# Fewer stretches of small products, a third pass one tile later, and five pieces of w_out in three passes

## The chip, the cores and the metric

The kernel runs on one core of one Trainium2 chip. The time is the device time of that core in microseconds. TensorE multiplies, VectorE (DVE in the profile) and ScalarE (ACT) work on the elements, GpSimd (POOL) does almost nothing here, and SyncE (SP) issues the transfers. The kernel before takes 519.27 us, the median of three runs from 519.05 to 519.50 us.

## The reference

Two blocks follow each other. The first is a recurrence over 768 steps, for 4 batches of 8 heads of width 48; its output is the input of a feed-forward layer with a squared ReLU.

```python
for t in range(S):
    state = alpha[:, :, t, :, None] * state + np.einsum('bhd,bhe->bhde', k[:, :, t], v[:, :, t])
    y[:, :, t] = np.einsum('bhd,bhde->bhe', q[:, :, t], state)
x = y.transpose(0, 2, 1, 3).reshape(B * S, H * D)      # 3072 x 384
h = np.maximum(x @ w_in, 0.0)                          # 3072 x 2048
out = h * h @ w_out                                    # 3072 x 384
```

## The kernel before, in words

**The recurrence.** The sequence is cut into 24 blocks of 128 steps, numbered so that block n is chunk n // 4 of batch n % 4. For a block the kernel takes logarithms of alpha (`ln`), sums them along the steps with a product against a triangle (`cs`, in two parts from block 8 on, split by `sp`), and takes exponentials of both signs (`eb`, `ei`), with which q and k are scaled (`mq`, `mk`). TensorE turns q and k by products with the identity (`turn`), and ScalarE copies them out of PSUM (`kc`, `qc`). Then come the small products: `scores` (line 413) and `state_sums` (line 442) for a block, and the output y of a pair of blocks (line 393). y has three parts, the product of q with the two states and a first and a second half of the masked scores times v. The two halves write the same banks from different rows of the array, so an empty POOL instruction, named `passed`, stands between them: it waits for the last product of the first half, and the first product of the second half waits for it. On VectorE a block's scores are masked (`masked`, line 424), its sums are read (`sums_copied`, line 456), and the state is moved on (`next_state`, lines 477 and 479; the last chunk has no next state). For blocks from 16 on each of the last three is two instructions, before that one. `ev_part` copies y out of PSUM into x, the input of the feed-forward layer, in four parts of three copies.

**The feed-forward layer.** Four blocks make a group of 512 rows, and there are six groups, 0 to 5. In group 0 the first layer multiplies in plain fp32. From group 1 on each operand is split into rounded parts and a tile of the hidden layer takes three passes. `in_x` does two of them, six products that end in a ScalarE step on the bank; `in_y` adds the third, three products on the same bank; and `in_post` applies the squared ReLU. A tile is one of three kinds, A, M or D, which set how much of this ScalarE does and how much VectorE. In the loop over the 16 tiles `in_y` runs two tiles behind `in_x`, and `in_post` three behind.

**The second layer** takes w_out in eight pieces. A piece is either plain (`out_plain`, eight fp32 products a group) or goes in three passes (`out_x` with two passes, `out_y` with the third, 24 products a group). `k0` and `k1` are the numbers of three-pass pieces in groups 0 and 1; from group 2 on all eight are. A three-pass piece needs the hidden tiles split first, one ScalarE and two VectorE instructions each (`split_h`, `diff_h`, lines 701, 653, 648).

**The order.** Everything is written by hand in program order. The start is a list of words in `AT['first']`. After it, `weave` walks through the units of the two layers, adds up their costs (about 1.29 us to a unit), and puts an attention step ahead of the first unit that starts at or after the time it is due. The due times of a pair of blocks come from `attention`: turn at t + 6.5, `ga` (sums of the first block, then y of the pair before up to the first half) at t + `AT['ga']`, `gb` (the second half, then sums of the second block) at t + `AT['gb']`. These are three separate stretches of small products a pair. All PSUM tiles come from one pool of eight banks, `ps_att`; a new tile gets the bank that has been free the longest, and waits until its last reader is done. Transfers go down SyncE's queue in program order, and `move` holds one back until an earlier one has landed (`AT['thr']`, `AT['thrp']`).

```python
units.append((1.05, in_x, (n,)))
units.append((0.53, in_y, (n - 2,)))
units.append((0, in_post, (n - AT["post"],)))
```

Of the kernel before, what the change touches and what calls it, by code (L numbers as in the profile page):

```python
# [18 lines left out]


GB = 4
AT = {'thrp': 4.5, 'cvo': 3.35, 'thr': 2.25, 'm48': 16, 'cvs': 3.9, 'cv1': 0.125, 'later': (0, 0, 4, 6, 0, 1, 0), 'evs': 0.1, 'lead': 4, 'post': 3, 'w_first': (46.0, 38.0, 49.0), 'wstep': 1.0, 'w_in_at': 2.5, 'w_in_by': 3.6, 'room1': 22, 'room': 24, 's0': 4, 'ahead': 6, 'late': 2, 'xs': 0.0, 'g0': ((0.5, 4, False, True, 27.75), (25.75, 6, True, True), (29.25, 8, True, False)), 'sc0': (3.25, 2.35, 2.35), 'g1': ((5.5, 8, False, 15.0), (13.0, 10, True), (35.25, 12, True)), 'g': ((2.075, 6, True), (14.25, 8, True)), 'g1x': 51.0, 'gx': 48.75, 'g0x': 56.25, 'k0': 2, 'h0': 15, 'k1': 4, 'h1': 3, 'h1by': 2, 'evs0': 0.7, 'tp': 'ADMD', 'tp1': 'ADAD', 'split': 8, 'o0': (46.5, 48.5), 'o1': (), 'o2': (21.25, 24.75, 24.5, 40.0, 35.25, 28.25), 'str1': 21.5, 'ga': 9.75, 'gb': 12.5, 'cv0': -1.25, 'pre': '1a 0a 0q 0k 1k 1q', 'cp': ('q2a', 'k2b', 'k0a', 'k3a', 'k3b', 'k0b', 'q0b', 'q3b', 'q2b', 'q3a'), 'evd': ((0, 0, 0), (0, 0, 1), (0, 1, 2), (0, 1, 3), (2, 0, 3), (2, 1, 1), (2, 1, 2)), 'first': 'ln0 load1v cs0 ei0 eb0 zeros4 mk0 mq0 qT0 kT0 ln1 cs1 kc0 ei1 warm0 load0v eb1 mk1 qc0 weights0 lt1 sc0 load2a mq1 load2q kT1 kc1 qT1 load2k load3a qc1 load3k kv0 am0 first0 load3v sc1 ln2 kv1 load3q us0 am1 weights6 us1 cs2 ya0 ei2 second0 eb2 lt0 ln3 yb0 load2v mq2 qT2 mk2 load4a ep00 ep01 qc2 kT2 cs3 kc2 eb3 ei3 zeros1 sc2 ep02 mq3 mk3 kT3 ep03 weights2 first1 st0 ha0 second1 lt2 kv2 am2 qT3 load4k kc3 qc3 ha1 weights5 first2 sc3 kv3 am3 load4q us2 ha2 us3 ya2 yb2 weights3 ep20 ep21 ep22 load4v ep23 second2 first3 weights1 st1 weights4 ha3 lt3 hb0 st2 second3 hb2 hb3 hb1 st3'}


RUN = {0: 128, 32: 32, 64: 64, 96: 32}
# [3 lines left out]
def kernel(  # L29
# [12 lines left out]
    nc = tc.nc  # L42
    B, H, S, D = q.shape
# [211 lines left out]
    def work(name, bufs=1):  # L255
        return p2.tile([128, NP, C], FP32, tag=name, name=name, bufs=bufs)
# [279 lines left out]
    def joined(a, n):  # L536
# [28 lines left out]
                    dep(begin, passed)  # L565
        next_state(n + 1)

    def turn(n):

        for m in (n, n + 1):  # L570
            need(("qb", m), ("kb", m))
            given.add(("free", "q", m))
            ps = blk[m]["T"] = [bank(m, "T", (2, NP, 64)) for _ in range(2)]
            for i, x in enumerate("kq"):
                rows = tile_of(x, m).rearrange("a h d -> a (h d)")
                for p in range(NP):
                    for h in range(2):
                        nc.tensor.transpose(  # L578
                            out=ps[h][:, i, p, :], in_=rows[HALF[h], 128 * p : 128 * (p + 1)],
                            identity=ident[HALF[h], HALF[h]],  # L580
                        )

    def turned_copied(x, n):
        t = blk[n][f"{x}s"] = work(f"{x}s", 2 if x == "k" else 4)
        for h in range(2):
            nc.scalar.copy(out=t[:, :, HALF[h]], in_=blk[n]["T"][h][:, "kq".index(x)])

    def ev_part(n, p):
        if p < NP - 1:
# [6 lines left out]
    def ev(n, ps=tuple(range(NP))):  # L596
        g, t = divmod(n, GB)
        need(("y", n))
        if ps[-1] == NP - 1:
            given.add(("x", n))  # L600
        if t == 0 and ps[0] == 0:
            if g == 0:
                xT[g] = [wt("x", shape=(GB * C,)) for _ in range(KM)]
            else:
                x = raw_pool.tile([128, KM, GB * C], FP32, tag="raw", name="x")
                xT[g] = [x[:, kk] for kk in range(KM)]
        x = [x.rearrange("a (t c) -> a t c", c=C) for x in xT[g]]

        for p in ps:
            for e, f, end in ((1, 2 * p * D + 32, 2 * (p + 1) * D), (0, 2 * p * D, (2 * p + 1) * D)):  # L610
                copy = nc.vector.tensor_copy if (n, e, p) in AT["evd"] else nc.scalar.copy
                r = 64 * (e ^ p % 2)
                while f < end:
                    kk, to = divmod(f, 128)
                    m = min(end - f, *(RUN[i % 128] for i in (r, to)))
                    copy(  # L616
                        out=x[kk][to : to + m, t : t + 2],
                        in_=blk[n]["y"][e][r : r + m, :, p // 2],
                    )
                    r, f = r + m, f + m  # L620
        if ps[-1] == NP - 1:
            blk[n].pop("y")
# [146 lines left out]
    def splits_of_x(at, g):  # L769
        return [(at + i * AT["xs"], f, (g, i % KM)) for i, f in enumerate((split_x,) * KM + (diff_x,) * KM)]  # L770

    def layer_in(g):
        units = []
        for n in range(NJ + 2):
            if n < NJ:
                units.append((1.05, in_x, (n,)))
            if 0 <= n - 2 < NJ:
                units.append((0.53, in_y, (n - 2,)))
            if 0 <= n - AT["post"] < NJ:
                units.append((0, in_post, (n - AT["post"],)))  # L780
            if AT["lead"] <= n < AT["lead"] + AHEAD and (g > 1 or AT["k1"] == NW):
                units += splits_of_h(0, n - AT["lead"])
        return units

    AHEAD, MORE = 3, 4
    h_parts, h_diff, extra = {}, {}, []

# [80 lines left out]
                used("d", "o", p)  # L868

    def layer_out(g):  # L870
        posts = [(0, in_post, (n,)) for n in range(NJ + 2 - AT["post"], NJ)] if g else []
        plain = NW - AT["k0"] if g == 0 else NW - AT["k1"] if g == 1 else 0
        first = 2 * plain
        units = [(1, out_plain, (p, t, plain)) for p in range(plain) for t in range(GB)]
        if plain:
            for i, x in enumerate(posts):
                units.insert(1 + 2 * i, x)
            posts = []
        if plain == NW:
            for t in range(GB):  # L880
                units.append((0, lambda t: store(g, t, out_tile(t)), (t,)))
            return units
        ahead = AT["ahead"]
        split = [f for i in range(0 if plain else AHEAD, NJ - first) for f in splits_of_h(first, i)]
        if g == 0:
            split = [f for i in range(NJ - first) for f in [(0, split_h, (first + i, 0)), (0, diff_h, (first + i,))]]
        if plain:
            at = AT["h0" if g == 0 else "h1"]
            for i in range(min(AHEAD, len(split) // 2)):
                units[at:at] = split[0:2]  # L890
# [115 lines left out]
    def attention(t, n0, after, scale=1, begun=True, whole_at=None, turn_at=None):  # L1006
# [41 lines left out]
                        loads(w + later[6], (n + 2, "a"))  # L1048
        return sorted(out, key=lambda x: x[0])

    def weave(units, events, at):
# [74 lines left out]
    for g in range(1, NG):  # L1126
# [52 lines left out]
```

## Time and profile before

| | |
|---|---|
| median of three runs | 519.27 us (519.05 to 519.50) |
| the profiled execution | 520.38 us, of which the span is 518.6 us |
| granted clock of TensorE | 1.000 |
| TensorE busy with products | 507.8 us, 98% of the span |
| VectorE, ScalarE | 355.7 us (69%), 306.4 us (59%) |
| transfers | 102.34 MB, 197 GB/s over the span |

A line of the timeline reads: start, length, engine, source line, operation, what is written from what, shape, and how many records it merges; in brackets the idle time before and what ended it. Matmuls are pipelined, so the length of one is not its price: the price is the distance from one start to the next. An fp32 product has two records, and one on rounded parts has one. In the chain of waits a line is start, length, engine, tile, source line and count.

### The profile page before, as it was taken

What the parts mean: (1) busy time and instruction counts of PE and PEld (TensorE: products, weight loads), DVE (VectorE), ACT (ScalarE), POOL (GpSimd) and SP (SyncE); (2) the same over time, 40 slices, a digit from 0 to 9 for tenths busy, and PEclk for the clock granted to TensorE, in tenths of its full rate; (3) what the DMA queues carried; (4) which work ended last, traced back from release to release, by engine and by line L of the source; (5) the groups of instructions that cost most, each with busy time, mean ns of one, the idle gap of its engine ahead of it and who ended that gap; (6) DMA issues with size and microseconds to landing.
All of it is one profiled execution on the core that took longest, in us unless ns stands there. A gap on an engine that the chain in (4) does not pass through costs nothing.

```text
span 518.6 us, 13019 instructions
## 1 busy us (share of the span) xinstructions
PE 507.8 (98%) x5338; PEld 418.9 (81%) x5338; DVE 355.7 (69%) x628; ACT 306.4 (59%) x649; POOL 5.3 (1%) x29
## 2 busy tenths in 40 slices
PE   7899999999999999999999999999999999999997
PEld 5675455678888669987899988899988899988997
DVE  2766669986887877776697468587465487363861
ACT  4788898547888653485664276772275673164620
POOL 4000000000000000000000000000000000000000
PEclk9999999999999999999999999999999999999999
DMA  9999779472777786898884688864683545699201
GB/s 183 204 267 237 197 189 235 93 228 80 238 190 184 246 243 162 265 279 227 205 225 143 222 247 222 223 200 152 213 274 124 185 121 154 207 380 322 65 2 61
DMA packets 139323, 102.34 MB, mean 197 GB/s; under 512 B 109808, under 2 KB 115968, under 8 KB 139264
## 3 DMA queue, kind: packets, MB, share of 16 engines
q1 hardware_dynamic: 139264, 101.51, 68.2%
q8 instruction: 42, 0.69, 0.6%
q14 instruction: 17, 0.14, 0.1%
HBM read 84.16 MB, written 17.33 MB: 196 GB/s over the span
## 4 chain that ended last, share of the span: by engine, by line
PE 93%; DVE 4%; issue 1%; POOL 1%; ACT 1%; DVEq 0%; POOLq 0%
PE o L809 39%; PE h L726 32%; PE h L919 8%; PE y L393 4%; PE sckv L413 2%; PE T L578 2%; PE sckv L442 2%; PE cs L283 1%; PE cs L286 1%; DVE x L616 1%; PE cs L287 1%; DVE hd L648 1%; DVE hx L653 0%; DVE am L424 0%; ACT x L616 0%
## 5 line engine op out<-in xcount | busy, mean ns | idle before, releaser
L726 PE MATMUL h<-xd,wd 128*128 128x512 f32 x240 | 68.1, 396 | 1.1 <-issue 1.1
L726 PE MATMUL h<-xa,wb 128*128 128x512 f32 x240 | 68.7, 394 | 0.0
L726 PE MATMUL h<-xl,wl 128*128 128x512 f32 x240 | 67.9, 391 | 0.0
L648 DVE TENSOR_TENSOR hid<-h,hid 128x512 f32<-128x512 f32 x40 | 27.6, 689 | 51.1 <-PE h L726 51.0
L616 ACT COPY x<-y 48x256 f32<-48x256 f32 (+3 forms) x133 | 46.7, 365 | 21.2 <-PE y L393 18.8
L809 PE MATMUL o<-wb,ha 128*128 128x384 f32 x160 | 54.5, 340 | 0.0
L743 ACT ACTIVATE h<-h 128x512 f32<-128x512 f32 x40 | 23.3, 582 | 52.3 <-PE h L726 52.3
L809 PE MATMUL o<-wl,hl 128*128 128x384 f32 x160 | 53.7, 336 | 0.1
L809 PE MATMUL o<-wd,hd 128*128 128x384 f32 x304 | 53.7, 334 | 0.0
L809 PE MATMUL o<-w_out,hid 128*128 128x384 f32 x160 | 53.6, 489 | 0.0
L726 PEld LDWEIGHTS h<-xl,wl 128*128 128x128 f32 x240 | 45.1, 188 | 10.1 <-DVE xl L653 0.4
L809 PEld LDWEIGHTS o<-wd,hd 128*128 128x128 f32 x304 | 52.8, 188 | 0.0
L726 PEld LDWEIGHTS h<-xa,wb 128*128 128x128 f32 x240 | 44.4, 188 | 9.8 <-ACT hid L763 0.4
L726 PEld LDWEIGHTS h<-xd,wd 128*128 128x128 f32 x240 | 44.0, 188 | 9.1
L809 PE MATMUL o<-wb,hx 128*128 128x384 f32 x144 | 48.3, 336 | 0.0
L809 PE MATMUL o<-wl,hx 128*128 128x384 f32 x144 | 48.1, 334 | 0.0
L809 PEld LDWEIGHTS o<-w_out,hid 128*128 128x128 f32 x160 | 30.0, 190 | 19.7
L741 ACT ACTIVATE hid<-h 128x512 f32<-128x512 f32 x40 | 24.2, 606 | 32.9 <-PE h L726 32.5
L919 PE MATMUL h<-x,w_in 128*128 128x512 f32 (+1 forms) x120 | 43.4, 512 | 0.2 <-DVE x L616 0.2
L701 ACT ACTIVATE ha<-hid 128x512 fp32r<-128x512 f32 x40 | 25.1, 642 | 20.3 <-PE o L809 7.9
L919 PEld LDWEIGHTS h<-x,w_in 128*128 128x128 f32 x120 | 22.1, 190 | 17.8 <-issue 15.3
L653 DVE SCALAR_TENSOR_TENSOR hl<-ha,hid 128x512 fp32r<-128x512 f32 x40 | 27.5, 687 | 6.9 <-ACT ha L701 6.8
(111 smaller groups left out, 852.5 us busy)
## 6 DMA issues: line engine op xcount, KB each, us to landing
wd<-do SPq DMA_DIRECT2D x36, 384.0 KB
wl<-lo SPq DMA_DIRECT2D x34, 384.0 KB
wl<-li SPq DMA_DIRECT2D x32, 384.0 KB
wd<-di SPq DMA_DIRECT2D x32, 384.0 KB
raw<-in_moe_w_out_dram SPq DMA_DIRECT2D x8, 767.5 KB
raw<-in_moe_w_in_dram SPq DMA_DIRECT2D x8, 767.2 KB
v_in<-in_v_dram SPq DMA_DIRECT2D x24, 192.0 KB
out_dram<-osb SPq DMA_DIRECT2D x24, 192.0 KB
```

The source lines that it names most:

```text
L393: ins = nc.tensor.matmul(out=ys[e][64 * half : 64 * half + D + G * e, m % 2, p // 2, t], lhsT=lhsT, rhs=rhs, start=(half, e) not in seen, ...
L413: nc.tensor.matmul(out=ps[e][HALF[h], 0, p, :], lhsT=ks[rows, p, HALF[h]], rhs=qs[rows, p, HALF[h]], start=True, stop=True, skip_group_che ...
L442: nc.tensor.matmul(out=ps[h][64 * e : 64 * e + m, 1, p, G:64], lhsT=tile_of("k", n)[HALF[h], 2 * p + e, 0:m], rhs=tiles["v"][n % NV][HALF[ ...
L616: copy(out=x[kk][to : to + m, t : t + 2], in_=blk[n]["y"][e][r : r + m, :, p // 2],)
L648: nc.vector.tensor_tensor(out=o, in0=x, in1=z, op=op)
L653: nc.vector.scalar_tensor_tensor(out=o, in0=x, scalar=c, in1=y, op0=ALU.mult, op1=op)
L701: nc.scalar.activation(out=a, in_=x, func=AF.Copy, scale=NEAR * E)
L726: nc.tensor.matmul(out=acc["h", j], lhsT=here[w, "i", p][:, kk, jj * 128 : (jj + 1) * 128], rhs=x_parts[x][:, kk], start=start and kk == 0 ...
L741: nc.scalar.activation(out=hid[j], in_=x, func=AF.Copy, scale=E)
L743: nc.scalar.activation(out=x, in_=x, func=AF.Copy, scale=1.0 + E)
L809: nc.tensor.matmul(out=acc[t][:, 0:DM], lhsT=lhs[:, t * C : (t + 1) * C], rhs=rhs, start=start, stop=stop, skip_group_check=True,)
L919: nc.tensor.matmul(out=ps, lhsT=w[:, kk, c0 : c0 + 128], rhs=xT[g][kk][:, cols], start=(kk == 0), stop=(kk == KM - 1),)
```

## The change

Four parts, all in the order of the work, and one in how many pieces go which way.

1. **Two stretches instead of three.** From group 2 on (`AT['ty']` is 2) a pair that has a pair before it goes through the new `attention_of_two`. `turn_and_y` does y of the old pair up to the first half, then the turn of the new pair, then the second half. `both_sums` does the scores and sums of both new blocks in one stretch, and after it the VectorE steps of both. It touches five pairs (first blocks 14, 16, 18, 20, 22); the last one (24) has no new pair and keeps its two stretches, earlier than before. The four `ev_part`s of a pair, which came 0.1 units apart behind `gb`, start 1.25 or 2.25 units behind the turn and come 1.6 units apart.
2. **The third pass one tile later.** From group 2 on (`AT['lg']` is 2) `in_y` and `in_post` run one tile behind `in_x`. The last third pass of the layer goes behind the first `out_x` of the second layer.
3. **Five pieces of w_out in three passes** in group 1 instead of four (`k1`).
4. **Other order.** The list `first`, the due times, the order of loads, which of the early copies VectorE does (`cp`, `evd`), the kinds of tile, and the limits on transfers under way.

The entries of `AT` that the prediction speaks of:

| entry | before | after |
|---|---|---|
| `k1` | 4 | 5 |
| `lead` (tile at which the first hidden tiles are split) | 4 | 2 |
| `s0` (splits put ahead of the second layer) | 4 | 5 |
| `evs` | 0.1 | 1.6 |
| `g` (pairs of groups 2 to 4: t and first block) | (2.075, 6, True), (14.25, 8, True) | (1, 6, True, 4.0, 1.25), (13, 8, True, 2.125, 2.25) |
| `ga`, `gb` | 9.75, 12.5 | 9.5, 12.5 |
| `gx` (split of the next group's x) | 48.75 | 44.5 |
| `tp` (kinds of four tiles) | ADMD | DMAD |
| `thr`, `thrp` | 2.25, 4.5 | 2.0, 7.0 |
| `cv1` (second step of a weight conversion behind the first) | 0.125 | 3.125 |
| `later` (loads behind ga, gb, turn, cs) | (0, 0, 4, 6, 0, 1, 0) | (0, 3, 1, 12, 3, 0, 1) |
| `o2` (preparing six pieces of w_out in group 1) | (21.25, 24.75, 24.5, 40.0, 35.25, 28.25) | (8.5, 19.25, -2.25, 32.25, 28.25, 39.5) |
| `evd` (early copies of y on VectorE) | (0,0,0) (0,0,1) (0,1,2) (0,1,3) (2,0,3) (2,1,1) (2,1,2) | (0,0,0) (0,0,1) (0,0,2) (0,0,3) (0,1,1) (0,1,3) (2,0,3) (2,1,0) (2,1,1) (2,1,2) |

In the list `first`, `lt0` goes ahead of `cs2`, the loads of block 3's alpha and k ahead of block 2's q and k, `zeros1` (two products that fill time) goes away, and `st1`, `st2` and `ha2` go ahead of the last `yb2`.

```diff
+    def turn_and_y(a, n):
+        if a is not None:
+            product = y_begin(a)
+            for h in range(2):
+                for m, p, e in heads(a):
+                    rows = slice(64 * e, 64 * e + D)
+                    s = blk[m]["u" if h else "s"]
+                    product(m, p, e, s[rows, p, G * (1 - e) : 64], blk[m]["qs"][rows, p, HALF[h]], HALF[h])
+            for m, p, e in heads(a):
+                end = inner(product, m, p, e, e)
+            passed = nc.gpsimd.nop(nofuse=True)
+            dep(passed, end)
+        if n is not None:
+            turn(n)
+        if a is not None:
+            for i, (m, p, e) in enumerate(heads(a)):
+                begin = inner(product, m, p, e, 1 - e)
+                if i == 0:
+                    dep(begin, passed)
+
+    def both_sums(n):
+        for m in (n, n + 1):
+            scores(m)
+            state_sums(m)
+        for m in (n, n + 1):
+            for f in (masked, sums_copied, next_state):
+                f(m)
...
+    def lags(g):
+        return (AT["lag"], AT["post2"]) if g >= AT["lg"] else (2, AT["post"])
+
     def layer_in(g):
         units = []
-        for n in range(NJ + 2):
+        lag, post = lags(g)
+        for n in range(NJ + lag):
+            if n == NJ and lag == 1:
+                left.append(units)
+                units = []
             if n < NJ:
                 units.append((1.05, in_x, (n,)))
-            if 0 <= n - 2 < NJ:
-                units.append((0.53, in_y, (n - 2,)))
-            if 0 <= n - AT["post"] < NJ:
-                units.append((0, in_post, (n - AT["post"],)))
+            if 0 <= n - lag < NJ:
+                units.append((0.53, in_y, (n - lag,)))
+            if 0 <= n - post < NJ:
+                units.append((0, in_post, (n - post,)))
...
         for n in range(first, NJ):
             units.append((1.08, out_x, (n, first)))
+            if left and n == AT["rest"]:
+                units += left.pop()
...
+    def attention_of_two(t, n0, gs=4.0, evy=1.5):
+        out = []
+        later = AT["later"]
+        old, new = n0 - 2, n0 if n0 < NBLK else None
...
+        w = t + 6.5
+        if new is None:
+            out += [(w - 1, ga, (old, None)), (w, gb, (old, None))]
+        else:
+            out.append((w, turn_and_y, (old, new)))
+        for p in range(NP):
+            out.append((w + evy + AT["evs"] * p, ev_part, (old, p)))
...
+        w = t + gs + 6.5
+        out.append((w, both_sums, (n0,)))
...
+                if g >= AT["ty"] and after:
+                    events += attention_of_two(at0 + t, n0, *other)
+                    continue
```

More of the change, by code (lines that the diff above doesn't have):

```diff
@@ new lines @@
+AT = {'tc': 'AAAA', 'rest': 0, 'lg': 2, 'lag': 1, 'post2': 1, 'ty': 2, 'thrp': 7.0, 'cvo': 2.6, 'thr': 2.0, 'm48': 16, 'cvs': 3.55, 'cv1': 3.125, 'later': (0, 3, 1, 12, 3, 0, 1), 'evs': 1.6, 'lead': 2, 'post': 3, 'w_first': (48.25, 39.25, 52.0), 'wstep': 1.6, 'w_in_at': 1.75, 'w_in_by': 3.6, 'room1': 23, 'room': 24, 's0': 5, 'ahead': 9, 'late': 2, 'xs': 0.0, 'g0': ((4.25, 4, False, True, 33.25), (23.75, 6, True, True), (28.0, 8, True, False)), 'sc0': (1.55, 2.35, 2.35), 'g1': ((5.5, 8, False, 16.5), (15.75, 10, True), (32.0, 12, True)), 'g': ((1, 6, True, 4.0, 1.25), (13, 8, True, 2.125, 2.25)), 'g1x': 52.0, 'gx': 44.5, 'g0x': 56.25, 'k0': 2, 'h0': 17, 'k1': 5, 'h1': 4, 'h1by': 2, 'evs0': 0.75, 'tp': 'DMAD', 'tp1': 'MAAD', 'split': 8, 'o0': (45.75, 47.25), 'o1': (), 'o2': (8.5, 19.25, -2.25, 32.25, 28.25, 39.5), 'str1': 21.0, 'ga': 9.5, 'gb': 12.5, 'cv0': 1.125, 'pre': '1a 0a 0q 0k 1k 1q', 'cp': ('k3b', 'k0b', 'q2b', 'k1b', 'q1a', 'q3b', 'k2b', 'k2a'), 'evd': ((0, 0, 0), (0, 0, 1), (0, 0, 2), (0, 0, 3), (0, 1, 1), (0, 1, 3), (2, 0, 3), (2, 1, 0), (2, 1, 1), (2, 1, 2)), 'first': 'ln0 cs0 ei0 eb0 mk0 zeros4 mq0 qT0 kT0 ln1 kc0 load1v cs1 ei1 warm0 eb1 load0v mk1 qc0 lt1 weights0 load2a sc0 load3a kT1 mq1 kc1 load3k qT1 load2q qc1 kv0 am0 us0 sc1 kv1 first0 load2k ln2 load3q lt0 weights6 load2v am1 us1 cs2 eb2 second0 mq2 ya0 ei2 yb0 mk2 ln3 qT2 ep00 ep01 kT2 qc2 cs3 kc2 load3v eb3 sc2 ei3 mq3 weights2 mk3 ep02 kT3 first1 load4q ep03 ha0 qT3 kc3 kv2 qc3 lt2 ha1 st0 second1 am2 us2 sc3 first2 load4a kv3 load4k ha2 weights5 am3 weights3 us3 ya2 st2 st1 weights1 weights4 yb2 ep20 ep21 ep22 ep23 first3 ha3 second2 load4v second3 lt3 st3 hb2 hb0 hb3 hb1'}
@@ L584, in turned_copied @@
         t = blk[n][f"{x}s"] = work(f"{x}s", 2 if x == "k" else 4)
+        i = "kq".index(x)
+        copy = nc.vector.tensor_copy if AT["tc"][2 * (n % 2) + i] == "D" else nc.scalar.copy
         for h in range(2):
-            nc.scalar.copy(out=t[:, :, HALF[h]], in_=blk[n]["T"][h][:, "kq".index(x)])
+            copy(out=t[:, :, HALF[h]], in_=blk[n]["T"][h][:, i])
     def ev_part(n, p):
@@ L610, in ev @@
             for e, f, end in ((1, 2 * p * D + 32, 2 * (p + 1) * D), (0, 2 * p * D, (2 * p + 1) * D)):
-                copy = nc.vector.tensor_copy if (n, e, p) in AT["evd"] else nc.scalar.copy
+                copy = nc.vector.tensor_copy if (n if n < GB else -1, e, p) in AT["evd"] else nc.scalar.copy
                 r = 64 * (e ^ p % 2)
@@ L770, in splits_of_x @@
         return [(at + i * AT["xs"], f, (g, i % KM)) for i, f in enumerate((split_x,) * KM + (diff_x,) * KM)]
+    def lags(g):
+        return (AT["lag"], AT["post2"]) if g >= AT["lg"] else (2, AT["post"])
     def layer_in(g):
         units = []
-        for n in range(NJ + 2):
+        lag, post = lags(g)
[3 more added lines that the diff above has]
+                units = []
             if n < NJ:
                 units.append((1.05, in_x, (n,)))
-            if 0 <= n - 2 < NJ:
-                units.append((0.53, in_y, (n - 2,)))
-            if 0 <= n - AT["post"] < NJ:
-                units.append((0, in_post, (n - AT["post"],)))
+            if 0 <= n - lag < NJ:
+                units.append((0.53, in_y, (n - lag,)))
+            if 0 <= n - post < NJ:
+                units.append((0, in_post, (n - post,)))
             if AT["lead"] <= n < AT["lead"] + AHEAD and (g > 1 or AT["k1"] == NW):
                 units += splits_of_h(0, n - AT["lead"])
+        if left:
+            left.append(units)
+            units = left.pop(0)
         return units
+    left = []
     AHEAD, MORE = 3, 4
@@ L870, in layer_out @@
     def layer_out(g):
-        posts = [(0, in_post, (n,)) for n in range(NJ + 2 - AT["post"], NJ)] if g else []
+        lag, post = lags(g)
+        posts = [(0, in_post, (n,)) for n in range(NJ + lag - post, NJ)] if g else []
         plain = NW - AT["k0"] if g == 0 else NW - AT["k1"] if g == 1 else 0
@@ L877, in layer_out @@
                 units.insert(1 + 2 * i, x)
+            if left:
+                units[1:1] = left.pop()
             posts = []
@@ L1049, in attention, with loads @@
         return sorted(out, key=lambda x: x[0])
+    def attention_of_two(t, n0, gs=4.0, evy=1.5):
+        out = []
+        later = AT["later"]
+        old, new = n0 - 2, n0 if n0 < NBLK else None
+        def loads(at, *which):
+            out.extend((at, load, (m, x)) for m, x in which if m < NBLK)
+        w = t + 6.5
[5 more added lines that the diff above has]
+            out.append((w + evy + AT["evs"] * p, ev_part, (old, p)))
+        loads(w + later[1], (n0 + 2, "v"))
+        loads(w + later[2], (n0 + 3, "v"))
+        if new is None:
+            return sorted(out, key=lambda x: x[0])
+        loads(w + later[4], (n0 + 2, "q"))
+        loads(w + later[5], (n0 + 3, "q"))
+        for at, fs in PLAN:
+            for f in fs.split():
+                if f not in ("turn", "ga", "gb"):
+                    n = n0 + int(f[-1])
+                    out.append((w if f[:2] in ("kc", "qc") else t + at, steps[f[:-1]], (n,)))
+                    if f[:-1] == "cs":
+                        loads(t + at + later[6], (n + 2, "a"))
+        w = t + gs + 6.5
+        out.append((w, both_sums, (n0,)))
+        loads(w + later[0], (n0 + 3, "k"))
+        loads(w + later[3], (n0 + 4, "k"))
+        return sorted(out, key=lambda x: x[0])
     def weave(units, events, at):
```

1 line of the change is left out of this document (removed).

## The prediction

> **What bounds the kernel now.** I read the page first, then the chain of waits in order of time, then TensorE's timeline, and then busy times by stage.
>
> ```profile
> PE 507.8 (98%) x5338; PEld 418.9 (81%) x5338; DVE 355.7 (69%) x628; ACT 306.4 (59%) x649; POOL 5.3 (1%) x29
> PE 93%; DVE 4%; issue 1%; POOL 1%; ACT 1%; DVEq 0%; POOLq 0%
> ...
> 85.11 11.61 PE o L809 x36
> ...
> 237.97 1.11 issue
> ...
> 343.32 30.70 PE o L809 x176
> ```
>
> TensorE is the bound, so a change counts by the TensorE time that it removes and by the waits that it makes. Line 809 gives two prices: 11.61/36 = 0.3225 us for a record of a plain product (two records each) and 30.70/176 = 0.174 us for one product of a three-pass piece. The "issue" line is a wait that nothing in the profile explains; I come back to it.
>
> ```profile
> 307.31 0.84 PE L726 MATMUL h<-xl,wl 128*128 128x512 f32 x3
> 308.09 0.46 PE L578 MATMUL T<-ident,k_in 64*128 64x64 f32 x8
> 308.38 0.41 PE L578 MATMUL T<-ident,q_in 64*128 64x64 f32 x8
> 308.63 0.42 PE L578 MATMUL T<-ident,k_in 64*128 64x64 f32 x8
> 308.89 0.42 PE L578 MATMUL T<-ident,q_in 64*128 64x64 f32 x8
> 309.23 0.97 PE L726 MATMUL h<-xd,wd 128*128 128x512 f32 x3
> 310.04 0.85 PE L726 MATMUL h<-xa,wb 128*128 128x512 f32 x3
> 310.73 0.86 PE L726 MATMUL h<-xl,wl 128*128 128x512 f32 x3
> ```
>
> Here the starts are to be read. Three products take 0.685 us at their pace (310.04 to 310.73). From the due end of the first three (307.31 + 0.685 = 307.995) to the due start of the three after the stretch (310.04 - 0.685 = 309.355) are 1.36 us. The 32 records inside need four times 0.25 us, 1.01 us. So a stretch of small products costs 0.35 us beyond its work.
>
> ```profile
> 12.60 0.69 PE L413 MATMUL sckv<-qs,ks 48*64 48x64 f32 x32
> 13.22 0.66 PE L354 MATMUL kT<-ident,k_in 128*128 128x128 f32 x4
> 17.25 0.91 PE L283 MATMUL cs<-a_lent,causal_r 128*128 128x384 f32 x2 [1.06 <-ACT a_lent L261]
> 24.35 0.63 PE L354 MATMUL kT<-ident,qk_lent 128*128 128x128 f32 x4 [0.86 <-DVE qk_lent L302]
> 37.04 3.29 PE L919 MATMUL h<-x,w_in 128*128 128x256 f32 x14 [0.21 <-DVE x L616]
> ```
>
> TensorE waits up to 37.04 us. Behind that a walk through its starts finds only four waits over 0.25 us: two of 0.30 us in group 1's second layer (186.69 and 191.27), the 1.27 us at 237.6, and 0.26 us at 270.99, where group 2's second layer begins and the split `hl` is late.
>
> ```profile
> 169.00:214.00 45.00, 45.00 (x547) 35.39 (x546) 35.76 (x64) 23.45 (x57) 0.00 (x0) 1.00 0.76 224
> 214.00:257.00 43.00, 41.89 (x564) 34.37 (x566) 26.69 (x53) 29.61 (x70) 0.00 (x0) 1.00 0.89 237
> 295.00:338.00 43.00, 43.00 (x614) 35.38 (x613) 29.42 (x61) 30.08 (x70) 0.00 (x0) 1.00 0.83 229
> ```
>
> ```profile
> 314.67 0.78 DVE L424 COPY_PREDICATED am<-halves_mask,sckv 128x256 f32<-128x256 uint32 x2 [0.96 <-PE sckv L442]
> 315.34 0.73 DVE L456 TENSOR_TENSOR us<-sckv,s 48x192 f32<-48x192 f32 x2
> 316.10 0.74 DVE L477 TENSOR_TENSOR s<-sckv,us 48x192 f32<-48x192 f32 x2
> 316.87 0.72 DVE L479 TENSOR_TENSOR s<-s,last 48x192 f32<-48x192 f32 x2
> ```
>
> The stages are group 1's second layer and the first layers of groups 2 and 3; the columns are the length, PE, PEld, DVE, ACT, POOL, clock, transfer share, GB/s. VectorE and ScalarE are 62 to 79% busy. A block's VectorE steps behind its sums take from 314.67 to 317.61, 2.9 us.
>
> **The fifth three-pass piece in group 1.** It removes 8 plain products, 16 records x 0.3225 = 5.16 us, and adds 24 x 0.174 = 4.18 us: **-0.98 us** on the path. It adds two hidden tiles to split, 2 x (0.69 + 0.69) = 2.8 us of VectorE and 2 x 0.63 of ScalarE, and one more third part (384 KB) to be read back, into a stage where transfers have a share of 0.76. VectorE goes from 35.8 of 45 us to 38.5 of 44. Two waits of 0.30 us were there already at 79%. Between no wait and the whole 2.8 us, I take **+0.2**, nearest to those rows. The preparing of pieces moves (`o2`): its two VectorE and one ScalarE instruction a piece keep their number, and its two stores a piece stay in SP's queue.
>
> **Two stretches for three, five times.** Gone are five stretches, 5 x 0.35 = 1.75 us. But the turn now stands between two halves of y, and its tile is 64x128 where y's is 64x64. No row shows that neighbourhood. Between small products of one tile height the timeline shows no pause (scores alone, 313.56 to 314.07, 0.51 us for 32). From a 64-row tile to a 128-row one it does: 32 scores up to the transposes took 13.22 - 12.60 = 0.62 us, so 0.11, and 32 sums ahead of qT took 26.67 to 27.28, 0.61 where 199.09 to 199.54 show 0.45, so 0.16. The price of a switch lies between 0 and 0.16. I take 0.135, the mean of the two rows in which the tile changes: a pair wins 0.35 - 0.27 = 0.08, five pairs **-0.4** (between -1.75 and -0.15). [...] The POOL instruction has the turn's 1.0 us for cover; POOL has nothing else queued. Uncovered it cost about 0.35 us once (the y of 64 records at 32.22), so without cover the part would be +1.35.
>
> **Both blocks' sums at once.** At `both_sums` y holds two banks, the sums four, hidden tiles two: all eight. The next `in_x` but one needs the bank that the first block's `us` frees. From the stretch's start the first block's products end at 0.87, VectorE begins 0.24 later, and mask and us take 1.43: free at 2.55 us. TensorE asks for it after 1.75 of small products, about 0.25 of leaving and 0.69 of `in_y`: at 2.7. So 0.15 us to spare, if VectorE is free. It then has 5.9 us in one burst for blocks 14 to 19, with the D tiles' steps and `hl` queued behind it, and 3.0 for the last chunk. Without spare the price is one to two 0.69 us steps a stretch: 0 to 5.6 us in all (1.4 at each of three long bursts, 0.7 at two short). I take 0.15 at the long ones, **+0.45**, since the one wait before that VectorE caused at such a place was 0.26.
>
> **The third pass a tile later.** From the end of `in_x` to its `in_y` there were 18 products, 4.1 us; now nine, 2.05 us. ScalarE's step on the bank takes 0.58, so 1.45 is left for what is ahead of it: eight turned copies (308.83 to 311.05, 2.2 us), four exponentials (1.5), or three copies of y (1.1). The copies begin while TensorE is still in the stretch, 1.2 us before it leaves, so they fit; 0, and if they don't, 0.65 us a time, up to 3.3. The second pair's copies of y, 4.3 us, move into the first layer: ScalarE 30 to 34 of 42 us. The four banks of T are free by then. One hidden tile less is alive.
>
> **Loads and other queues.** Counts on SP's queue are unchanged but for the piece above: a pair still issues eight loads, two rows out and four `last` in. The k load at the sums has 6 units, 7.7 us, to the next `mk`; behind it stand the parts of w_in and w_out. Transfers have a share of 0.83 to 0.89 there and TensorE waited for none: 0. If that cover went, a load of some 1 us late would cost as much, once a pair.
>
> **The start.** The chain of first conversion (ACT 14.88), second conversion (DVE 17.18 to 20.03), scaling of q and its transposes at 20.73 keeps its order, and so do block 3's exponentials ahead of the transposes at 24.35. What changes is the last copying of y (33.77 to 36.98), 7 copies on ACT and 5 on DVE, now 5 and 7 with the two banks kept apart; TensorE waited 0.38 and 0.21 there. **-0.3**, between -2.5 (all the waits behind 16 us) and +2.5 (as much again). The later `hl` at 270.99 has two tiles more of `lead`: **-0.26**. In group 0 the second step of a conversion comes 3 units later and still 4 units before its piece is used: 0.
>
> **Sum**: -0.98 + 0.2 - 0.4 + 0.45 - 0.3 - 0.26 = **-1.3 us**. The profiled execution took 520.38 us, its span 518.6 with 1.8 around it; that gives 519.1 for it. It lies 1.1 us above the median, just the size of the unexplained wait, which I take for a guest of that execution. So the median goes from 519.27 to **518.0**.
>
> **The rivals.**
> *More is won.* Turn and y switch freely (-1.35 more) and the bank waits stay away (-0.45): 516.2. For it: no pause between small products of one tile height. Against: the 0.11 and 0.16.
> *Nothing measurable.* Two switches and the bank waits eat the stretches, and group 1's VectorE takes half of the piece back: 518.0 + 0.4 + 0.5 = 518.9.
> *Slower: banks held by VectorE.* All eight are taken and the longest-free one is still being read; 0.9 us at each of five stretches is 4.5 in place of 0.45, 522.0. For it: 0.15 us of spare and 68% busy VectorE. Against: before, with seven banks taken, it waited only 0.26. It decides from 0.55 us a stretch on (2.75 - 0.45 = 2.3 over 518.0).
>
> **How the numbers follow.** As summed, 517.3 to 518.2: 0.33. More won, 515.5 to 517.3: 0.22. Within 0.2% (1.04 us, about what a measurement of this kernel can tell): 0.20. Slower, 520.3 to 524: 0.25. Faster is the first two, 0.55. Leaving out 0.05 below and 0.14 above gives 516.0 to 521.8; the likeliest alone is 517.3 to 518.2.
>
> **What would show it.** Records of line 809 on w_out fall from 160 to 144 and three-pass ones rise by 24. In groups 2 to 4 the transposes stand between two y parts; their neighbours' starts give the switch. TensorE's idle time behind `both_sums`, ended by DVE `us` or `s`, should be under 0.2 us. A wait of `in_y` for ACT's step on h (lines 741, 743, 763) would prove me wrong on the third pass, and one before 40 us on the start.

## The result and the profile after

The changed kernel takes **520.16 us** (median of 22 executions, 518.75 to 522.87) against 518.79 us before (22 executions, 518.23 to 519.55). The ratio is 1.0028 with an interval of 1.0017 to 1.0038: 0.28% slower, where 0.2% faster was forecast. The time lies inside the range that was given, on the wrong side of the kernel before.

The 22 times are not one heap. Sorted by the mean granted clock of TensorE: eight executions at 1.000 take 518.75 to 519.18 us (median 518.97), eleven at 0.996 or 0.997 take 519.30 to 521.86, and three at 0.993 take 522.15 to 522.87. The executions at full clock are 0.2 us over the median of the kernel before, so most of the loss of 1.4 us lies in executions whose clock fell. The profiled execution of the changed kernel is one at full clock: 518.8 us with a span of 517.0.

From the page of the changed kernel, busy times and the chain that ended last:

```profile
PE 506.8 (98%) x5344; PEld 420.4 (81%) x5344; DVE 359.3 (69%) x632; ACT 309.8 (60%) x651; POOL 5.3 (1%) x29
...
PE 90%; DVE 4%; DMA 4%; ACT 1%; issue 1%; SPq 0%; DVEq 0%; POOLq 0%; ACTq 0%
```

TensorE is busy 1.0 us less, about what the fifth piece was to save. New in the chain is "DMA 4%": before, no transfer stood in it. Its pieces are loads of alpha, k and v in the start, so the start is the place to look. SyncE's queue of the kernel before (start, length, queue, line, what is loaded, count), and under it that of the changed kernel:

```profile
0.74 1.05 SPq L109 DMA_DIRECT2D a_in<-in_alpha_dram  x2
1.84 0.85 SPq L109 DMA_DIRECT2D q_in<-in_q_dram  x1
2.73 1.96 SPq L109 DMA_DIRECT2D k_in<-in_k_dram  x2
...
8.56 0.41 SPq L109 DMA_DIRECT2D raw<-in_moe_w_in_dram  x1
```

```profile
0.74 1.06 SPq L109 DMA_DIRECT2D a_in<-in_alpha_dram  x2
1.85 0.60 SPq L109 DMA_DIRECT2D q_in<-in_q_dram  x1
3.37 1.57 SPq L109 DMA_DIRECT2D k_in<-in_k_dram  x2
...
9.26 0.37 SPq L109 DMA_DIRECT2D raw<-in_moe_w_in_dram  x1
```

Before, the fourth load goes out at 2.73 us; in the changed kernel it is held until 3.37. That is `AT['thr']`, 2.25 before and 2.0 after: `move` counts a load of alpha, q, k or v as 1.1, so four of them are under way against three. All loads behind it are late too, the first piece of w_in (`raw`) by 0.70 us. Who waits for that piece, in the timelines of ScalarE and TensorE, first before and then after:

```profile
14.88 1.91 ACT L179 ACTIVATE power<-raw,rebias 128x768 uint16<-128x768 int16 x2
16.67 0.53 ACT L261 ACTIVATE a_lent<-a_lent 128x384 f32<-128x384 f32 x1
```

```profile
14.62 1.88 ACT L179 ACTIVATE power<-raw,rebias 128x768 uint16<-128x768 int16 x2 [0.43 <-DMA raw<-in_moe_w_in_dram]
16.41 0.51 ACT L261 ACTIVATE a_lent<-a_lent 128x384 f32<-128x384 f32 x1
...
16.97 0.91 PE L283 MATMUL cs<-a_lent,causal_r 128*128 128x384 f32 x2 [1.12 <-ACT a_lent L261]
```

ScalarE converts the piece (line 179) before it takes block 2's logarithm (line 261), and TensorE's sum `cs` of block 2 waits for the logarithm. Before, ScalarE came to the conversion without a wait. Now it is there sooner, since its steps ahead come earlier, and waits 0.43 us for the piece. TensorE's wait at `cs` is 1.12 us, hardly more than the 1.06 of before: at this place the execution loses nothing yet.

The stages on TensorE, each from its first product to that of the next:

| stage | before | after | |
|---|---|---|---|
| start and group 0 | 126.17 | 126.25 | +0.08 |
| group 1 | 87.91 | 86.51 | -1.40 |
| group 2 | 80.87 | 79.66 | -1.21 |
| group 3 | 78.91 | 79.72 | +0.81 |
| group 4 | 75.10 | 75.28 | +0.18 |
| group 5 | 69.64 | 69.60 | -0.04 |

By these two executions 1.6 us are won. But the one of before had taken 520.38, 1.6 over the median of its 22 executions. The pair of profiles shows where time moved; it can't show the loss, as neither has a fallen clock. It also makes the start look level; why that is not to be relied on stands in the section on the prediction.

The new neighbourhood of y and the turn, in TensorE's timeline of the changed kernel at the first of the five pairs:

```profile
225.48 0.68 PE L393 MATMUL y<-am,v_in 64*48 64x64 f32 x31
226.09 0.46 PE L606 MATMUL T<-ident,k_in 64*128 64x64 f32 x8
226.39 0.41 PE L606 MATMUL T<-ident,q_in 64*128 64x64 f32 x8
226.64 0.42 PE L606 MATMUL T<-ident,k_in 64*128 64x64 f32 x8
226.89 0.42 PE L606 MATMUL T<-ident,q_in 64*128 64x64 f32 x8
227.24 0.69 PE L393 MATMUL y<-am,v_in 64*48 64x64 f32 x32
227.87 0.97 PE L756 MATMUL h<-xd,wd 128*128 128x512 f32 x3
228.67 0.85 PE L756 MATMUL h<-xa,wb 128*128 128x512 f32 x3
```

Record by record, the last y ahead of the turn and the first transpose start 0.149 us apart, the last transpose and the next y 0.154, at all five pairs alike; inside a run the neighbours are some 0.015 apart for y and 0.032 for the transposes. Both switches of tile are paid, with about 0.13 and 0.12 us.

### The profile page after: what moved, and what is told of

It reads as the page before. It is cut to its first block, busy times and chain, and to the rows that moved or that the text cites. A ratio compares the mean times of both kernels' runs of the same rounds, so it can differ in the third digit from the quotient of the medians.

```text
span 517.0 us, 13038 instructions
## 1 busy us (share of the span) xinstructions
PE 506.8 (98%) x5344; PEld 420.4 (81%) x5344; DVE 359.3 (69%) x632; ACT 309.8 (60%) x651; POOL 5.3 (1%) x29
## 4 chain that ended last, share of the span: by engine, by line
PE 90%; DVE 4%; DMA 4%; ACT 1%; issue 1%; SPq 0%; DVEq 0%; POOLq 0%; ACTq 0%
PE o L850 39%; PE h L756 32%; PE h L965 8%; PE y L393 5%; PE T L606 2%; PE sckv L413 2%; PE sckv L442 2%; DMA k_in<-in_k_dram 1%; DMA a_lent<-in_alpha_dram 1%; DVE x L646 1%; DVE hd L678 1%; DMA a_in<-in_alpha_dram 1%; PE cs L283 1%; PE cs L287 1%; DMA v_in<-in_v_dram 1%; PE cs L286 1%
## 5 line engine op out<-in xcount | busy, mean ns | idle before, releaser
L850 PE MATMUL o<-wb,ha 128*128 128x384 f32 x168 | 57.4, 341 | 0.2 <-DVE s L477 0.2
L850 PE MATMUL o<-wl,hl 128*128 128x384 f32 x168 | 56.5, 336 | 0.3 <-DVE hl L683 0.3
L646 ACT COPY x<-y 32x256 f32<-32x256 f32 (+2 forms) x129 | 46.3, 364 | 15.8 <-PE y L393 11.6
L756 PEld LDWEIGHTS h<-xa,wb 128*128 128x128 f32 x240 | 44.5, 188 | 9.6 <-issue 0.5
L771 ACT ACTIVATE hid<-h 128x512 f32<-128x512 f32 x36 | 21.6, 599 | 45.8 <-PE h L756 45.0
L850 PE MATMUL o<-w_out,hid 128*128 128x384 f32 x144 | 49.0, 491 | 0.0
L773 ACT ACTIVATE h<-h 128x512 f32<-128x512 f32 x44 | 25.6, 582 | 38.3 <-PE h L756 36.5
L678 DVE TENSOR_TENSOR hid<-h,hid 128x512 f32<-128x512 f32 x36 | 24.8, 688 | 31.6 <-PE h L756 31.4
L850 PEld LDWEIGHTS o<-w_out,hid 128*128 128x128 f32 x144 | 26.8, 190 | 17.6 <-issue 0.5
L731 ACT ACTIVATE ha<-hid 128x512 fp32r<-128x512 f32 x42 | 26.8, 637 | 21.7 <-DVE hx L683 10.7
L850 PEld LDWEIGHTS o<-wb,ha 128*128 128x128 f32 x168 | 31.5, 188 | 1.5 <-PE o L850 0.5
```

The source lines that it names most:

```text
L646: copy(out=x[kk][to : to + m, t : t + 2], in_=blk[n]["y"][e][r : r + m, :, p // 2],)
L678: nc.vector.tensor_tensor(out=o, in0=x, in1=z, op=op)
L731: nc.scalar.activation(out=a, in_=x, func=AF.Copy, scale=NEAR * E)
L756: nc.tensor.matmul(out=acc["h", j], lhsT=here[w, "i", p][:, kk, jj * 128 : (jj + 1) * 128], rhs=x_parts[x][:, kk], start=start and kk == 0 ...
L771: nc.scalar.activation(out=hid[j], in_=x, func=AF.Copy, scale=E)
L773: nc.scalar.activation(out=x, in_=x, func=AF.Copy, scale=1.0 + E)
```

## The experiments

Three theories. **A**: the joined stretch (y, turn, y, then both blocks' sums) leaves TensorE short of work in groups 2 to 4, and the clock falls there. **B**: the clock falls in the start. **C**, which came up behind the first runs: of what the change does to the start, the limit on transfers under way is the cause.

**The changed kernel once more**, with no edit.

> The changed kernel once more, for its spread and for the place where the granted clock falls. It took 518.75 to 519.18 us in the executions whose mean granted clock was 1.000 and 519.3 to 522.9 us where it was 0.993 to 0.997. Theory A (the joined stretch): y, the turn and y again are one stretch of 3.3 us of small products, and in some executions the clock falls to half behind one of them for about 3.4 us (0.0033 of the span, about 1.7 us); the windows of the profile would show a clock below 1 within groups 2 to 4, just behind a y, T, y stretch. Theory B (the start): the clock falls in the first 40 us, where TensorE waits. Median 520.2 us by both, about half of the executions below a clock of 1.

Measured: 519.59 us against 519.01 (ratio 1.0015, 0.9993 to 1.0038). The clock fell below 0.999 in 6 of 12 executions, and in 1 of 23 of the kernel before. This time the profile caught one with a fallen clock (0.997, 520.24 us). Stretches of it, with length, then PE, PEld, DVE, ACT and POOL busy, and the granted clock third from the end:

```profile
16.00:18.00 2.00, 0.37 (x1) 0.30 (x2) 0.96 (x3) 1.78 (x5) 0.00 (x0) 1.00 0.65 130
18.00:19.00 1.00, 1.00 (x14) 0.33 (x16) 0.96 (x2) 0.22 (x1) 0.00 (x0) 0.60 1.19 239
19.00:20.00 1.00, 1.00 (x50) 1.00 (x46) 0.97 (x2) 1.00 (x3) 0.00 (x0) 0.50 1.13 208
20.00:21.00 1.00, 0.87 (x34) 0.69 (x30) 1.00 (x3) 0.06 (x1) 0.00 (x0) 0.50 0.87 162
21.00:22.00 1.00, 1.00 (x34) 0.93 (x31) 0.07 (x1) 0.10 (x1) 0.00 (x0) 0.69 0.93 215
22.00:23.00 1.00, 1.00 (x9) 0.89 (x8) 0.70 (x2) 0.95 (x3) 0.00 (x0) 1.00 0.91 332
...
214.00:294.00 80.00, 79.82 (x923) 71.59 (x923) 57.12 (x106) 45.92 (x103) 0.00 (x0) 1.00 0.77 226
294.00:374.00 80.00, 79.75 (x890) 71.33 (x890) 55.98 (x103) 45.92 (x103) 0.00 (x0) 1.00 0.70 206
```

The clock is 1.00 through all joined stretches and half between some 18.2 and 21.6 us. What is missing sums to 0.40 + 0.50 + 0.50 + 0.31 = 1.71 us, which is 0.0033 of the span: just the step from 1.000 to 0.997. Ahead of it stands the same wait as above, longer:

```profile
15.31 1.85 ACT L179 ACTIVATE power<-raw,rebias 128x768 uint16<-128x768 int16 x2 [1.39 <-DMA raw<-in_moe_w_in_dram]
17.06 0.51 ACT L261 ACTIVATE a_lent<-a_lent 128x384 f32<-128x384 f32 x1
...
17.63 1.11 PE L283 MATMUL cs<-a_lent,causal_r 128*128 128x384 f32 x2 [2.05 <-ACT a_lent L261]
```

For this execution A falls and B stands. Group 1 begins at 127.63 us instead of 126.25, the stages behind it are the same to 0.03 us, and that is the loss.

**Three stretches a pair again**, with the third pass still one tile behind `in_x`. (That is what the title calls one tile later: in the kernel before it is two behind.)

```diff
-'ty': 2, 'evs': 1.6, 'ga': 9.5, 'g': ((1, 6, True, 4.0, 1.25), (13, 8, True, 2.125, 2.25))
+'ty': 99, 'evs': 0.1, 'ga': 9.75, 'g': ((2.075, 6, True), (14.25, 8, True))
```

> The changed kernel, but the pairs of groups 2 to 4 go through three stretches again, with the due times of before (g, ga, evs). Theory A: no execution with a clock below 1, 518.5 to 519.0 us, and no wide spread. Theory B: the start is unchanged, so about half of the executions stay below a clock of 1, median 520 us.

Measured: 539.07 us, ratio 1.038 (1.0355 to 1.0405). The due times of before and the third pass one tile behind don't go together: the scores get a bank that a hidden tile still holds. TensorE's timeline:

```profile
263.83 0.28 PE L413 MATMUL sckv<-qs,ks 48*64 48x64 f32 x2
269.40 1.02 PE L413 MATMUL sckv<-qs,ks 48*64 48x64 f32 x27 [5.29 <-DVE hid L678]
```

A second wait like it follows at 352.10. As a price of the stretches the run decides nothing. But its start is that of the changed kernel and no stretch is joined, and in its profile the clock is still half from 17.6 to 21.0 us, behind a wait of 1.64 us at `cs`: B again. In the wait of 5.29 us the clock falls too, and is 0.50 from 267 to 273 us, which shows the same half clock at another place.

**Two stretches alone in the kernel before**, with its third pass two tiles behind.

```diff
-'ty': 99, 'g': ((2.075, 6, True), (14.25, 8, True))
+'ty': 2, 'g': ((1.075, 6, True, 4.0, 1.25), (13.25, 8, True, 2.125, 2.25))
```

> The kernel before, but the pairs of groups 2 to 4 go through two stretches; start, k1, the third pass two tiles behind and everything else are as before. Theory A: the clock falls below 1 in about half of the executions, which then take 1 to 4 us longer; those at a clock of 1 take 518.8 to 520 us (the joining itself gains nothing: each of the two switches between y and T costs 0.14 us, as much as the stretch saved). Theory B: every execution at a clock of 1, 518.8 us.

Measured: 548.17 us, ratio 1.057 (1.0534 to 1.0605). At each of the five turns TensorE's timeline has this:

```profile
226.81 0.41 PE L606 MATMUL T<-ident,q_in 64*128 64x64 f32 x8
228.24 0.73 PE L606 MATMUL T<-ident,k_in 64*128 64x64 f32 x8 [1.01 <-ACT qs L616]
```

The second block's part of the turn gets no bank until ScalarE has copied the first block's q out (`qs`, line 616). These are 5.1 of the 29 us; more waits of the kind stand at the scores (6.3 us). The due times differ as well, so the next run takes the one thing alone.

**The changed kernel with the third pass two tiles behind**, as it was before.

```diff
-'lg': 2, 'lead': 2
+'lg': 99, 'lead': 4
```

> The changed kernel with the third pass two tiles behind again (lg out of reach, lead 4), two stretches a pair kept. With one more hidden tile alive the eight banks do not hold y, the turn and the tiles: TensorE waits inside the turn, 1.2 us at each of five pairs as in the kernel before with two stretches, and at the sums 0.7 to 3: 528 to 545 us. If the banks are not the reason, 519.6 to 520.5 us.

Measured: 537.83 us, ratio 1.036 (1.0337 to 1.0382). The wait at the turn is there again, and one at the sums too:

```profile
227.15 0.73 PE L606 MATMUL T<-ident,k_in 64*128 64x64 f32 x8 [1.01 <-ACT qs L616]
...
236.08 0.63 PE L413 MATMUL sckv<-qs,ks 48*64 48x64 f32 x27 [1.11 <-DVE us L456]
```

The profile's waits of these two kinds sum to 5.1 and 6.0 us. So parts 1 and 2 of the change are one: the third pass one tile behind sets free the bank that two stretches need, and without it they cost 18 us.

**Only the fifth piece in the kernel before.**

```diff
-'k1': 4
+'k1': 5
```

> The kernel before, with five pieces of w_out in three passes in group 1 and nothing else. If the working holds: 5.16 us of plain products out, 4.16 in, 1.0 us less, less up to 0.2 for waits on VectorE: 517.8 to 518.0 us, all at a clock of 1. If VectorE in group 1 takes it back: 518.8.

Measured: 521.92 us, ratio 1.006 (1.004 to 1.0079), where a gain was expected. Group 1 takes 89.25 us instead of 87.91, with waits that were not there:

```profile
193.88 0.47 PE L606 MATMUL T<-ident,q_in 64*128 64x64 f32 x8 [0.97 <-DVE q_in L302]
...
207.37 0.62 PE L850 MATMUL o<-wd,hd 128*128 128x384 f32 x2 [0.40 <-DVE osb L887]
...
237.75 0.96 PE L756 MATMUL h<-xa,wb 128*128 128x512 f32 x3 [1.24 <-DVE lo L274]
```

The second layer is shorter by the piece, so the turn falls due sooner than VectorE has scaled q. The piece wins its microsecond only with the due times of part 4 beside it. The third wait lies in group 2, where the piece changes nothing; in the kernel before the same three products start at 235.98, ahead of its `lo` (236.67), so `lo` is hardly what they wait for, and the cause stays open. Three of the 12 executions fell below 0.999 as well, with the start and the limit of before; the profiled one did not, so where they fell isn't known.

**Only the limit on transfers, both ways.** First the changed kernel with the limit of before, then the kernel before with the new limit.

```diff
-'thr': 2.0
+'thr': 2.25
```

> The changed kernel with the limit on transfers under way (thr) at 2.25 again instead of 2.0, nothing else. Theory C (transfers under way): with 2.0 a load of nominal 1.1 waits until all but two earlier ones have landed, with 2.25 all but three; so three are under way at the start instead of four, the first piece of w_in is issued 0.7 us later (9.26 against 8.56 us), ScalarE's first conversion waits for it (14.62 and 15.31 us) with the logarithm of block 2 queued behind it, TensorE is idle 1.1 to 2.2 us before block 2's sums, and the clock falls behind that in some executions. By C the clock stays at 1 in nearly all executions and the median is 518.0 to 518.7 us. Theory D (the list): the new order of the list first is the cause, whatever thr is: about half of the executions below a clock of 1, median 519.6 to 520.2 us.

Measured: 518.45 us against 519.11, ratio 0.9988 (0.9977 to 0.9998), no execution of 11 below 0.999. So the new order of the list alone, its theory D, does not make the clock fall. Its timelines show no wait for the piece, and half the idle time in front of `cs`:

```profile
14.17 1.92 ACT L179 ACTIVATE power<-raw,rebias 128x768 uint16<-128x768 int16 x2
15.96 0.53 ACT L261 ACTIVATE a_lent<-a_lent 128x384 f32<-128x384 f32 x1
...
16.55 0.91 PE L283 MATMUL cs<-a_lent,causal_r 128*128 128x384 f32 x2 [0.61 <-DVE us L456]
```

> The kernel before with thr at 2.0 instead of 2.25, nothing else. Theory C: the first piece of w_in is issued 0.7 us later, TensorE waits longer around 16 us, about half of the executions fall below a clock of 1, median 519.5 to 520.5 us. Theory D: no change, 518.9 us, clock 1 in nearly all.

Measured: 519.77 us, ratio 1.0025 (1.0008 to 1.0042), which is as much as the whole change loses. The way is only partly the same. Two of 12 executions fell to 0.992, but the others are later too (median 519.5 at full clock against 519.07). In the profile, at full clock, ScalarE reaches the conversion at 14.62 us and the piece is there; group 1 begins at 125.89 us. With the limit of before, the same start began it at 126.17 us (the kernel before), 125.99 (two stretches alone) and 125.19 (only the fifth piece), so a single profile can't tell a few tenths here. Behind the start it has one wait over 0.3 us:

```profile
269.40 0.34 PE L850 MATMUL o<-wb,ha 128*128 128x384 f32 x1
270.62 0.45 PE L850 MATMUL o<-wl,hl 128*128 128x384 f32 x1 [0.89 <-DVE hl L683]
```

What else the lower limit costs in that order stays open.

**Block 2's logarithm ahead of the conversion**, the limit left at 2.0: if the piece is late, let the logarithm not stand behind it.

```diff
-kv1 first0 load2k ln2
+kv1 ln2 first0 load2k
```

> The changed kernel with the logarithm of block 2 (ln2) ahead of the first weight conversion (first0) in the list, thr still 2.0. If what holds TensorE at 16 us is the logarithm queued behind a conversion that waits for its piece, block 2's sums no longer wait: TensorE's idle time before them falls from 1.1 to 2.2 us to under 0.5, the clock stays at 1 in most executions and the median is 518.3 to 519.0 us. If the alpha of block 2 itself lands late, nothing changes: 519.6 to 520.2 us.

Measured: 521.73 us, ratio 1.0053 (1.0034 to 1.0073): a miss. ScalarE's timeline shows why:

```profile
16.05 0.52 ACT L261 ACTIVATE a_lent<-a_lent 128x384 f32<-128x384 f32 x1 [2.26 <-DMA a_lent<-in_alpha_dram]
16.48 1.86 ACT L179 ACTIVATE power<-raw,rebias 128x768 uint16<-128x768 int16 x2
```

Block 2's alpha lands later still than the piece of w_in did (16.05 us here, against 14.62 and 15.31 in the profiles above), and now the conversion stands behind it. TensorE's wait at `cs` is 1.18 us, but q of block 2 and what follows come later: group 1 begins at 129.09 us. Seven of eight executions fell below full clock. In the profile the clock is near a half from 18 to 25 us; the missing clock sums to 3.4 us, twice the 1.71 us above.

**The limit at 2.0, 2.25 and 3.0 side by side**, on a third chip.

> The changed kernel unchanged, so that the two others stand beside it on one chip. Theory C (three loads under way in place of four at the start): 519.0 to 520.5 us, between 0.1% and 0.4% over the kernel before; mean clock below 0.999 in a third or more of its executions.

> The changed kernel with thr 2.25 once more, on another chip. Theory C: 518.2 to 518.8 us, 0.1% to 0.35% under the unchanged changed kernel beside it, and the clock below 0.999 in at most one execution in ten. If the gain of the first time was that chip's: within 0.1% of the unchanged one, with as many executions at a lower clock.

> The changed kernel with thr 3.0, one load more under way than with 2.25. Theory C, if what counts is when the first piece of w_in lands: as with 2.25 or up to 0.3 us better, 517.9 to 518.8. If what counts is not to have too many under way (each then takes longer): the first block's q and k come later and it is worse by 0.3 to 1 us, 518.8 to 519.8.

| limit | median us (12 each) | ratio to before (518.93) | below 0.999 |
|---|---|---|---|
| 2.0 | 518.90 | 1.0011 (0.9994 to 1.0028) | 4 |
| 2.25 | 518.57 | 0.9992 (0.998 to 1.0004) | 0 |
| 3.0 | 518.59 | 0.9986 (0.9975 to 0.9997) | 0 |

In the three measurements of the changed kernel the clock fell in 14 + 6 + 4 = 24 of 46 executions. With the limit at 2.25 or 3.0 it fell in none of 35, and the kernel before in 2 of the 77 whose clock is known. Side by side on this chip it is 4 of 12 against 0 of 24. The medians differ less than expected here, 0.33 us or 0.06%, since the median execution of the 2.0 has full clock this time. The run with 3.0 is no test of a fifth load: three loads count 3.3, so 3.0 holds the next one just as 2.25 does, and lets one more out only behind a piece of weights, which counts 2.3 (block 2's alpha goes out at 10.58 us, against 11.10 and 11.17 with 2.25). C holds for the clock of the changed kernel. Its version with 2.25 or 3.0 is the fastest here, 0.1% ahead of before; for one of the three measurements the interval includes no gain.

## Why the prediction was wrong

**The start: the step that failed.** It put the start at -0.3 us: the chain of conversion, scaling and transposes "keeps its order", and the copies of y win a little. Neither gave the time it promised. First, the copies lost instead of winning. From group 0's first product to group 1's, the four profiles with the order of before take 101.36 us and the nine with the new order 101.78 to 101.81, whatever the limit: 0.43 us more for the same products. TensorE's timeline, before and after:

```profile
24.82 1.46 PE L919 MATMUL h<-x,w_in 128*128 128x256 f32 x6
```

```profile
24.48 1.03 PE L965 MATMUL h<-x,w_in 128*128 128x256 f32 x4
25.71 0.67 PE L965 MATMUL h<-x,w_in 128*128 128x256 f32 x2 [0.20 <-DVE x L646]
```

At their pace of 0.216 us four records bring the next one to 25.34; it starts at 25.71. These 0.36 us are a wait for VectorE's copies of y, which was not there before, ahead of the place where the gain was sought. Second, it matters when the data land, and not only in what order the steps stand: `thr` stood in the table of entries and got no price. The step on loads looked at queue counts in groups 2 to 4 alone, and found them unchanged. Group 1 begins at 126.23 to 126.25 us in three profiles with 2.0 whose clock is full there, at 125.75, 126.00 and 125.87 with 2.25 and 3.0: 0.2 to 0.5 us for the limit. And no term of the sum was for the clock: where it fell, group 1 begins at 127.63, and the median execution, a fallen one, is 1.2 us over the full-clock median (520.16 against 518.97). The prediction did name the place where it would be proved wrong, "one before 40 us on the start". Its bound of +2.5 for the start covers the loss, but the chances treated it as a gain.

**The fifth piece**: the records of plain products fell from 160 to 144, and the -0.98 came. The +0.2 for VectorE did not; the two waits of 0.30 us stand as they were, now at 182.54 and 185.82. Four pauses of 0.1 us at 126 went as well, together -1.40. But it was costed as a part by itself, and by itself it loses 0.6%.

**The stretches**: -0.4 forecast. Over five pairs the small products, with the way out of them, take 0.78 us longer (two switches each), entering costs 0.47 less, and five slow first triples of 0.11 fall away: about -0.25. The two-switch reading was right, and the "more is won" rival, that turn and y switch freely, is out.

**Both blocks' sums**: +0.45 forecast. There is one such wait, 0.35 us at 258.86, ended by `s`. The rival that ended slower, banks held by VectorE, had the right sign and the wrong cause.

**The third pass**: 0 forecast, and no `in_y` of the changed kernel waits for ScalarE. That it is what makes room for the two stretches (18 us) was not seen.

**The later `hl`**: the -0.26 was read off a row that the unexplained wait had shortened. In the profile of the kernel before with the lower limit nothing stands at 237.6, and TensorE loses 1.05 us at this `hl` (269.40 to 270.62, less the pace of 0.17). Without the 1.27 us group 2 takes 80.39 us, only 0.48 less. The guess that they were a guest of that execution is not borne out: the run with only the fifth piece has an unexplained wait of like size 2 us earlier (237.75). The changed kernel waits at group 3's second layer in its place, in TensorE's timeline:

```profile
349.38 0.34 PE L850 MATMUL o<-wb,ha 128*128 128x384 f32 x1
349.97 0.44 PE L850 MATMUL o<-wl,hl 128*128 128x384 f32 x1 [0.25 <-DVE hl L683]
```

From 349.38 to 349.97 are 0.59 us against a pace of 0.17: 0.42 lost, half of what group 3 takes more. It recurs at 348.88 with the limit at 2.25.

**The base, and what is left.** The forecast of 518.0 took 1.3 us off a median of 519.27 from three executions. The 22 gave 518.79, so 0.5 us of the distance to the result is the base. Behind the start the sum held: groups 1 to 5 take 390.73 to 390.83 us in all seven profiles that have them as in the changed kernel, against 392.42 before and 391.90 before with the lower limit, so 1.1 to 1.7 less where 0.99 was forecast. The start took it back. The profile of before is 1.6 us over its median; 0.5 of that is its group 2 (80.87 against 80.39), so its start of 126.17 should be some 1.1 too long, and 125.1 us is an estimate for the median execution (125.19 was seen). Against that the changed start is about 1.1 us later at full clock, and 0.6 to 0.9 with the limit at 2.25 or 3.0. Of the 1.1, the copies are 0.43 and the limit 0.2 to 0.5; the remainder is within the spread of the starts and stays open.

## What to carry to other kernels

A limit on transfers under way belongs to the data path: before costing a change at the start, list for each first step the engine reaches when its data are issued, not only the order of the steps. One profile of a start that spreads by 1 us is no base for a term of 0.3. Look at the spread of the times and at the granted clock of every execution; when the median moves and the profile doesn't, the lost time sits in executions that were not profiled. Parts of a change that share banks or due times have no price of their own: two stretches with the third pass two tiles behind cost 18 us, the fifth piece without the moved due times 3 us.

## What the runs showed of the hardware

A wait of 2.05 us in the start of the changed kernel was followed by half clock for 3.42 us (1.71 us of clock missing), and then full clock again; with 3.4 us missing, in the run with block 2's logarithm ahead of the conversion, the mean clock is 0.993. Of the 13 profiles, the clock fell in the start in three, with waits of 2.05, 1.64 and 1.18 us at `cs`, and in none of the ten with 0.60 to 1.12. The step from 1.12 to 1.18 is small, so the length of this one wait need not be all that decides. The same program fell in 24 of its 46 executions, and the wait itself differs between its three profiles (1.03, 1.12 and 2.05 us); what decides besides the wait, no run here shows.

In this kernel, with TensorE 98% busy, one such fall with the late piece ahead of it costs 0.9 to 1.6 us: so far do the executions at 0.996 and 0.997 lie over those at full clock in the three measurements of the changed kernel, by their medians. That is about as much as the best part of this change wins (1.40 us in group 1).
